# Transposing dqkv for the dxn loop by DMA from SBUF, three tiles ahead, in place of PE

## The chip, the cores and the metric

One core of one Trainium2 chip runs the whole program. The metric is the device time of one execution in microseconds (us), as a median over several executions. The profiles are single executions; their span is 1.7 to 1.9 us shorter than the device time of the same execution. PE is the matmul engine, DVE the vector engine, ACT the scalar engine, SP the engine that only issues DMAs here; SPq and ACTq are the DMA-issuing entries of SP and ACT.

## The reference

The forward pass and the gradients of one pre-layernorm block: linear attention, then a SwiGLU MLP, with 2048 rows and a width of 640 (`S`, `D`). Outputs are the block's result and the gradients of the input and of five weights.

```python
def _fwd_reference(A_x, A_wqkv, A_wo, B_x, B_w1, B_w3, B_w2):
    ...
    x = A_x
    h = x + _A_ref(_layernorm(x, axis=-1), A_wqkv, A_wo)
    h2 = h + _B_ref(_layernorm(h, axis=-1), B_w1, B_w3, B_w2)
    return h2

def reference(A_x, A_wqkv, A_wo, B_w1, B_w3, B_w2, B_x, grad_out):
    ...
    _out, _vjp = jax.vjp(_f, A_x, A_wqkv, A_wo, B_w1, B_w3, B_w2)
    _grads = _vjp(grad_out)
    return (jnp.asarray(_out), *[jnp.asarray(_g) for _g in _grads])
```

The change concerns one product of the backward pass: dxn = dqkv · wqkvᵀ, with dqkv of 2048 x 1920, followed by the backward of the first layernorm.

## The kernel before

The gradients of q, k and v lie in SBUF as `g_q`, `g_k`, `g_v`, in 16 tiles of 128 rows. For dxn the contraction runs over the 1920 columns, so each tile has to be transposed: 15 blocks of 128 x 128. PE transposes five blocks into a PSUM tile, ACT (q and v) or DVE (k) copies them into `gT`. The transposes of tile t+1 stand between the 30 matmuls of tile t. One weight-gradient job of 16 matmuls (`grad_job`) stands ahead of each tile as long as there are any: 20 jobs, 6 of them ahead of the loop, so tiles 14 and 15 have none.

```python
    for i in range(SC):
        dma(out=hnN[:, i * TPC:(i + 1) * TPC, :], in_=hn_v[:, i * TPC:(i + 1) * TPC, :])
    load_block(0)
    load_block(1)
    gT = {}

    def e_T(t, k):
        if k == 0:
            gT[t] = ex.tile([P, 15, P], BF16, name="gT", bufs=2)
        tr = ps.tile([P, DT, P], BF16, name="trq", bufs=2)
        for c in range(DT):
            T.transpose(tr[:, c, :], gqkv[k][:, t, c * P:(c + 1) * P], ident[:])
        if k == 1:
            V.tensor_copy(out=gT[t][:, k * DT:(k + 1) * DT, :], in_=tr[:])
        else:
            A.copy(out=gT[t][:, k * DT:(k + 1) * DT, :], in_=tr[:])

    def e_gxn(t):
        acc = ps.tile([P, 2, 512], F32, name="gxn", tag="gxn", bufs=2)
        for j in range(2):
            for k in range(15):
                T.matmul(acc[:, j, 0:HD], lhsT=gT[t][:, k, :], rhs=wqT[:, k, j * HD:(j + 1) * HD],
                         start=(k == 0), stop=(k == 14))
                if j * 15 + k in (7, 15, 23) and t + 1 < ST:
                    e_T(t + 1, (j * 15 + k) // 8)
        gx = ex.tile([P, D], BF16, name="gx", bufs=2)
        ln_bwd(acc, t, xnN[:, t, :], ln1, gx[:], g_h[:, t, :], ex)()   # ACT sum, DVE, ACT scale, DVE add
        A.dma_start(out=out1S[:, t, :], in_=gx[:])
    # ... pools ...
    for k in range(3):
        next(jobs)
        next(jobs)
        e_T(0, k)
    for t in range(ST):
        next(jobs, None)
        e_gxn(t)
    # ... last stage: 60 jobs with hnN and the blocks gb, load_block(i + 2) at block i ...
```

## Time and profile before

| | before |
|---|---|
| device time, median of 3 | 919.74 us |
| span of the profile | 917.3 us |
| PE / DVE / ACT busy | 96% / 49% / 42% |
| dxn stage, first g_k job to first gb job (PE timeline) | 673.4 to 796.5 us, 123.1 us |
| PE per tile in the loop | 7.08 us |

The busy shares say that PE bounds the program. They do not say how close another engine is: ACT waits inside its sequence of a tile (2.01 us for DVE in the lines that are cut below), and a wait is not counted as busy. The timeline of ACT in one tile of the loop shows this (columns: start in us, length in us, engine, line, operation, output and input, count; in brackets the idle time before it and what ended it):

```profile
744.15 0.70 ACT L636 ACTIVATE gs<-gxn 128x640 bf16<-128x640 f32 x1
...
749.64 1.47 ACT L891 COPY gT<-trq 128x640 bf16<-128x640 bf16 x2 [0.41 <-ACT obs L800]
751.23 0.70 ACT L636 ACTIVATE gs<-gxn 128x640 bf16<-128x640 f32 x1
```

From one sum `gs` to the next it is 7.08 us, PE's pace, but after the two copies ACT stands idle for only 751.23 - 749.64 - 1.47 = 0.12 us. Of the 7.08 us it is busy 3.5; the rest are the waits for DVE in the middle of the layernorm backward and the issue of two stores.

### The profile page before, as it was taken

What the parts mean: (1) busy time and instruction counts of PE and PEld (TensorE: products, weight loads), DVE (VectorE), ACT (ScalarE), POOL (GpSimd) and SP (SyncE); (2) the same over time, 40 slices, a digit from 0 to 9 for tenths busy, and PEclk for the clock granted to TensorE, in tenths of its full rate; (3) what the DMA queues carried; (4) which work ended last, traced back from release to release, by engine and by line L of the source; (5) the groups of instructions that cost most, each with busy time, mean ns of one, the idle gap of its engine ahead of it and who ended that gap; (6) DMA issues with size and microseconds to landing.
All of it is one profiled execution on the core that took longest, in us unless ns stands there. A gap on an engine that the chain in (4) does not pass through costs nothing.

```text
span 917.3 us, 16861 instructions
## 1 busy us (share of the span) xinstructions
PE 883.4 (96%) x6729; PEld 611.5 (67%) x6757; DVE 449.0 (49%) x1146; ACT 388.7 (42%) x722; POOL 22.5 (2%) x42
## 2 busy tenths in 40 slices
PE   5999899999999999899999999999899999999998
PEld 3777554555555555677677777777677777777776
DVE  6776688888888677200145655555323443400000
ACT  3556777665565665011123223223334545422211
POOL 4000000000000000000000000000000000000000
PEclk9999999999999999999999999999999999999999
DMA  9678583353343552999444555148996011066861
GB/s 297 188 246 258 147 240 119 99 141 108 99 136 115 176 168 93 230 224 265 133 134 125 153 163 144 37 165 174 219 275 153 33 40 38 28 153 150 178 149 37
DMA packets 272447, 138.33 MB, mean 151 GB/s; under 512 B 173808, under 2 KB 271088, under 8 KB 272368
## 3 DMA queue, kind: packets, MB, share of 16 engines
q1 hardware_dynamic: 253856, 124.05, 51.8%
q10 hardware_dynamic: 18512, 13.20, 4.6%
q8 instruction: 53, 0.87, 0.4%
q14 instruction: 26, 0.21, 0.1%
HBM read 45.20 MB, written 50.02 MB: 104 GB/s over the span
## 4 chain that ended last, share of the span: by engine, by line
PE 82%; DVE 2%; DMA 2%; ACT 2%; issue 1%; ACTq 0%; DVEq 0%
PE job L796 20%; PE mm L400 19%; PE ghn L625 13%; PE gxn L897 7%; PE gw L559 7%; PE o L448 5%; PE h L675 2%; PE at L361 2%; PE gwo L716 2%; DMA hb<-hh_d 2%; PE trq L887 1%; DMA vaT<-va_d 1%; PE dkv L702 1%; PE h L702 1%; PE h1b L687 1%
## 5 line engine op out<-in xcount | busy, mean ns | idle before, releaser
L400 PE MATMUL mm<-hnT,w 128*128 128x512 bf16 x546 | 132.7, 379 | 1.7 <-ACT hnT L395 1.0
L796 PE MATMUL job<-gb,hnN 128*128 128x288 bf16 x960 | 117.8, 286 | 0.0
L796 PEld LDWEIGHTS <-hnN 128*128 128x128 bf16 x960 | 93.9, 98 | 23.7
L625 PEld LDWEIGHTS <-ggb 128*128 128x128 bf16 x864 | 82.4, 98 | 30.2 <-issue 0.5
L400 PEld LDWEIGHTS <-w 128*128 128x128 bf16 x560 | 53.8, 98 | 61.3 <-issue 1.1
L800 ACT CAST obs<-job 128x288 bf16<-128x288 f32 (+1 forms) x90 | 36.8, 409 | 132.9 <-PE job L796 88.0
L897 PE MATMUL gxn<-wqT,gT 128*128 128x320 bf16 x480 | 74.8, 299 | 0.0
L400 PE MATMUL mm<-g2T,w2T 128*128 128x512 bf16 x266 | 68.3, 379 | 0.8
L448 PE MATMUL o<-w,hhT 128*128 128x320 bf16 x448 | 67.9, 299 | 1.0 <-DVE h L453 1.0
L625 PE MATMUL ghn<-w13a,ggb 128*128 128x320 bf16 x448 | 67.8, 299 | 0.0
L559 PE MATMUL gw<-g,hb 128*128 128x320 bf16 (+1 forms) x448 | 61.1, 299 | 1.3 <-DMA hb<-hh_d 1.3
L219 PE MATMUL big<-wqkv,pqT 128*128 128x320 bf16 x400 | 59.6, 305 | 2.7 <-DVE kvacc L258 1.0
L625 PE MATMUL ghn<-w13b,ggb 128*128 128x320 bf16 x416 | 61.2, 299 | 0.0
L448 PEld LDWEIGHTS <-hhT 128*128 128x128 bf16 x448 | 43.8, 98 | 24.9 <-issue 1.2
L219 PEld LDWEIGHTS <-pqT 128*128 128x128 bf16 x480 | 46.4, 99 | 20.8 <-DVE kvacc L258 1.3
L412 ACT CAST ghh<-mm 128x512 bf16<-128x512 f32 x56 | 32.9, 588 | 63.3 <-issue 39.3
L796 PEld LDWEIGHTS <-xnN 128*128 128x128 bf16 x480 | 47.2, 99 | 18.5
L559 PEld LDWEIGHTS <-hb 128*128 128x128 bf16 (+1 forms) x448 | 44.1, 99 | 18.4 <-DMA hb<-hh_d 1.7
L897 PEld LDWEIGHTS <-gT 128*128 128x128 bf16 x480 | 45.1, 98 | 14.8
L636 ACT ACTIVATE gs<-ghn 128x640 bf16<-128x640 f32 x16 | 11.3, 705 | 95.8 <-PE ghn L625 95.8
L648 ACT ACTIVATE y<-wb,s,ln_rs 128x640 bf16<-128x640 f32 x32 | 29.4, 920 | 40.9 <-DVE wb L644 40.9
L420 ACT ACTIVATE sig<-mm 128x512 bf16<-128x512 f32 x56 | 33.4, 597 | 24.8 <-PE mm L400 24.1
(136 smaller groups left out, 1212.0 us busy)
## 6 DMA issues: line engine op xcount, KB each, us to landing
ggb<-gg_d SPq DMA_DIRECT2D x8, 1728.0 KB, 9.5
hh_d<-hhT SPq DMA_DIRECT2D x52, 128.0 KB, 1.8
gg_d<-gate SPq DMA_DIRECT2D x52, 128.0 KB, 1.9
gg_d<-sig SPq DMA_DIRECT2D x52, 128.0 KB, 1.8
out_dram<-obs ACTq DMA_DIRECT2D x60, 72.0 KB, 2.7
w<-in_B_w_dram SPq DMA_DIRECT2D x4, 864.0 KB, 5.5
va_d<-va SPq DMA_DIRECT2D x4, 768.0 KB, 6.5
out_dram<-gw2o ACTq DMA_DIRECT2D x18, 160.0 KB, 4.7
```

Of the source, the lines that this page charges most:

```text
L219: T.matmul(acc, lhsT=pqT[:, c, t * P:(t + 1) * P], rhs=wqkv[:, c, n0:n0 + HD], start=(c == 0), stop=(c == DT - 1))
L361: T.matmul(at[:, 0:HD], lhsT=oT[t][:, c, :], rhs=wo[:, c, j * HD:(j + 1) * HD], start=(c == 0 and not on_pe), stop=(c == DT - 1))
L400: T.matmul(acc[:], lhsT=w[:, c, fc * P:(fc + 1) * P], rhs=rhs[:, c, :], start=(c == 0), stop=(c == DT - 1))
L412: A.copy(out=ghh[fc][:], in_=acc[:])
L420: A.activation(sig[:], gp[:], AF.Sigmoid)
L448: T.matmul(o2["ps"][:, 0:HD], lhsT=hhT[c][:, fc, i * P:(i + 1) * P], rhs=w2[:, fc, j * HD:(j + 1) * HD], start=(fc == 0), stop=(fc == FT - 1))
L559: T.matmul(acc[:n, j, 0:HD], lhsT=hb[b][:, t, i * P:i * P + n], rhs=g2[:, t, j * HD:(j + 1) * HD], start=(t == 0), stop=(t == ST - 1))
L625: T.matmul(acc[:, j, 0:HD], lhsT=ggb[t // 2][:, k, lo:lo + P], rhs=rhs[:, j * HD:(j + 1) * HD], start=(k == 0), stop=(k == NG - 1))
L648: A.activation(out=y[:], in_=wb[:], func=AF.Identity, bias=s[:, 3:4], scale=st.rs[:, t:t + 1])
L796: T.matmul(acc[:, 0:n], lhsT=lhs[:, t, m * P:(m + 1) * P], rhs=rhs(t), start=(t == 0), stop=(t == ST - 1))
L800: A.copy(out=ob, in_=acc[:, 0:n])
L897: T.matmul(acc[:, j, 0:HD], lhsT=gT[t][:, k, :], rhs=wqT[:, k, j * HD:(j + 1) * HD], start=(k == 0), stop=(k == 14))
```

## The change

Its intent: PE is the bound and the DMA engines are nearly idle in this loop, so let a DMA transpose g_q, g_k and g_v from SBUF straight into `gT`, early enough to be hidden. `gT` gets a third buffer, tile t+3 is transposed after tile t, and the loads for the last stage move from ahead of the loop into it, so that they do not delay the first transposes. Two more switches in the diff (the same idea in two other loops) are off and change nothing; their hunks are cut.

```diff
+TR_A, TR_B, TR_E = 0, 0, 1
 ...
-    for i in range(SC):
-        dma(out=hnN[:, i * TPC:(i + 1) * TPC, :], in_=hn_v[:, i * TPC:(i + 1) * TPC, :])
-    load_block(0)
-    load_block(1)
+    def load_hnN():
+        for i in range(SC):
+            dma(out=hnN[:, i * TPC:(i + 1) * TPC, :], in_=hn_v[:, i * TPC:(i + 1) * TPC, :])
+
+    if not TR_E:
+        load_hnN()
+        load_block(0)
+        load_block(1)
 ...
-            gT[t] = ex.tile([P, 15, P], BF16, name="gT", bufs=2)
+            gT[t] = ex.tile([P, 15, P], BF16, name="gT", bufs=3 if TR_E else 2)
+        if TR_E:
+            dmaT(out=gT[t][:, k * DT:(k + 1) * DT, :], in_=gqkv[k][:, t, :])
+            return
 ...
-                if j * 15 + k in (7, 15, 23) and t + 1 < ST:
+                if j * 15 + k in (7, 15, 23) and t + 1 < ST and not TR_E:
 ...
+    if TR_E:
+        for t in (1, 2):
+            for k in range(3):
+                e_T(t, k)
+        load_hnN()
     for t in range(ST):
         next(jobs, None)
         e_gxn(t)
+        if TR_E:
+            for k in range(3):
+                if t + 3 < ST:
+                    e_T(t + 3, k)
+            if t in (5, 9, 13):
+                load_block((t - 5) // 4)
 ...
-        load_block(i + 2)
+        load_block(i + 2 + TR_E)
```

More of the change, by code (lines that the diff above doesn't have):

```diff
@@ L346, in f2_ot @@
     def f2_ot(t):
+        if TR_A and t >= TPC:
+            o_t, oT[t] = oT[t], pf.tile([P, DT, P], BF16, name="oT", bufs=2)
+            dmaT(out=oT[t][:], in_=o_t[:])
+            return
         tr = ps.tile([P, DT, P], BF16, name="tr", bufs=1)
@@ L391, in f2_ht @@
             hnT[c] = pf.tile([P, DT, W], BF16, name="hnT", bufs=2)
+        if TR_A and t >= TPC:
+            dmaT(out=hnT[c][:, :, i * P:(i + 1) * P], in_=hn[t][:])
+            return
         tr = ps.tile([P, DT, P], BF16, name="tr", bufs=1)
@@ L481 @@
     for i in range(TPC):
-        for k, pos, f in ((3 * i, 0, f2_ndo), (3 * i + 1, 1, f2_ot), (3 * i + 2, 1, f2_at), (3 * i + 3, 0, f2_hn),
-                          (3 * i + 4, 0, f2_ht)):
+        for k, pos, f in ((3 * i, 0, f2_ndo), (3 * i + (not TR_A), 1, f2_ot), (3 * i + 2, 1, f2_at),
+                          (3 * i + 3, 0, f2_hn), (3 * i + 3 + (not TR_A), TR_A, f2_ht)):
             side[pos].setdefault(k, []).append((f, i))
@@ L653, in b_ln, with by_dma @@
         ln_rest[t] = ln_bwd(acc, t, hnb[t][:], ln2, g_h[:, t, :], g2[:, t, :], br)
+    def by_dma(t):
+        return TR_B and t < ST - 2
     def b_gT(t):
+        if by_dma(t):
+            ghT[t] = br.tile([P, DT, P], BF16, name="ghT", bufs=2)
+            dmaT(out=ghT[t][:], in_=g_h[:, t, :])
+            return
         tr = h1b(DT)
@@ L684, in b_gndT @@
     def b_gndT(t):
+        if by_dma(t):
+            gndT[t] = br.tile([P, CT, P], BF16, name="gndT", bufs=2)
+            dmaT(out=gndT[t][:], in_=gnd[t][:])
+            return
         tr = h1b(CT)
@@ L742 @@
             load_gg(t // 2 + 1)
-        if 0 <= u < ST:
+        if 0 <= u < ST and not by_dma(u):
             b_gT(u)
@@ L748 @@
         if w >= 0:
-            b_gndT(w)
-            b_gkv(w)
+            if not by_dma(w):
+                b_gndT(w)
+            if not TR_B:
+                b_gkv(w)
         part()
-        if 0 <= u < ST:
+        if 0 <= u < ST and not TR_B:
             b_go(u)
@@ L756 @@
             ln_rest.pop(t - 1)()
+            if by_dma(t - 1):
+                b_gT(t - 1)
+        if w >= 0 and TR_B:
+            b_gkv(w)
         part()
-        if w >= 0:
+        if 0 <= u < ST and TR_B:
+            b_go(u)
+        if w >= 0 and not TR_B:
             b_gpq(w)
@@ L761 @@
         part()
+        if w >= 0 and TR_B:
+            b_gpq(w)
+        if 0 <= u < ST and by_dma(u):
+            b_gndT(u)
         if t == ST:
@@ L883, in e_T @@
         if k == 0:
-            gT[t] = ex.tile([P, 15, P], BF16, name="gT", bufs=2)
+            gT[t] = ex.tile([P, 15, P], BF16, name="gT", bufs=3 if TR_E else 2)
+        if TR_E:
+            dmaT(out=gT[t][:, k * DT:(k + 1) * DT, :], in_=gqkv[k][:, t, :])
+            return
         tr = ps.tile([P, DT, P], BF16, name="trq", bufs=2)
```

## The prediction

> **What bounds the kernel now.** I read the page first (busy shares, slices, DMA), then the PE timeline and the groups by shape of the stage that the change touches, then who waited for whom there, then the DMA queue. The change touches one stage only: the dxn loop (16 tiles, L897) with the six weight-gradient jobs ahead of it. The order of instructions of the two builds differs in nothing else that can matter: PE loses 480 of 13,516 rows (240 transposes with their weight loads), ACT 32 copies, DVE 16 copies, SP gains 48 transposes and has the loads of hnN and of the first gb blocks later; the kernel's two other switches are off.
>
> ```profile
> PE 883.4 (96%) x6729; PEld 611.5 (67%) x6757; DVE 449.0 (49%) x1146; ACT 388.7 (42%) x722; POOL 22.5 (2%) x42
> ...
> PE   5999899999999999899999999999899999999998
> ...
> DMA  9678583353343552999444555148996011066861
> ```
>
> PE is busy for 96% of the span and nine tenths or more in nearly every slice, while the DMA engines have four almost empty slices, 30 to 34 (some 690 to 800 us): the dxn loop. One tile of it, and its last two, from the PE timeline (start, length, what; the bracket is idle time with its releaser):
>
> ```profile
> 708.52 2.34 PE L796 MATMUL job<-g_k,xnN 128*128 128x320 bf16 x16
> 710.69 1.25 PE L897 MATMUL gxn<-wqT,gT 128*128 128x320 bf16 x8
> 711.78 0.44 PE L887 MATMUL trq<-ident,g_q 128*128 128x128 bf16 x5
> 712.06 1.25 PE L897 MATMUL gxn<-wqT,gT 128*128 128x320 bf16 x8
> ...
> 715.60 2.34 PE L796 MATMUL job<-g_v,xnN 128*128 128x320 bf16 x16
> ```
>
> ```profile
> 789.19 1.25 PE L897 MATMUL gxn<-wqT,gT 128*128 128x320 bf16 x8
> 791.36 0.44 PE L887 MATMUL trq<-ident,g_v 128*128 128x128 bf16 x5 [0.92 <-DVE gT L889]
> 791.64 5.05 PE L897 MATMUL gxn<-wqT,gT 128*128 128x320 bf16 x36
> ```
>
> Lengths overlap because matmuls are pipelined, so costs are read from one start to the next. Five transposes: 712.06 - 711.78 = 0.28 us. A job of 16: 710.69 - 708.52 = 2.17. Eight gxn: 1.09, 0.136 each. A tile: 715.60 - 708.52 = 7.08 us = 2.17 + 30 x 0.136 + 3 x 0.276. Nothing else is in it: PE is the bound, with no gap. The only wait of PE from 673 to 797 us is the bracket above: the last tiles have no job between them, and there a transpose waits for the copy that frees its PSUM buffer.
>
> The copies beside it, by shape, are not on the path:
>
> ```profile
> L891 ACT COPY gT<-trq 128x640 bf16<-128x640 bf16 x32 | 21.9, 692 | 11.3 <-ACT obs L800 6.7 <-PE trq L887 3.0 <-DVE gT L889 0.9
> ...
> L889 DVE COPY gT<-trq 128x640 bf16<-128x640 bf16 x16 | 7.9, 491 | 26.0 <-PE trq L887 26.0
> ```
>
> ACT and DVE are busy 3.53 and 2.89 us of the 7.10 us of this tile in the busy time by stretches, and wait between pieces. Taking their copies away gives time only through PE.
>
> **What the Trainium skill says.** "TensorE: Matmul & The Clock Gate", Part 4 (PE-mode transpose): a 128x128 transpose was measured at about 390 ns alone and 275 ns in a kernel. The trace has 219 ns as the length of one, but pipelined five start within 0.276 us, 55 ns each; the saving must be counted by the 55. The skill's figure or the 219 ns would promise 53 to 66 us for 240 of them, four times too much.
> "DMA: Bandwidth & Descriptors", Latency and other measured facts: DMA transposes move 261 GB/s with a non-contiguous middle dimension. Here 1.18 MB of a gb block take 4.84 us to issue (244 GB/s) and land after 7.7 us; that agrees.
> Same page, the passage on the B0 build under "Why a DMA increments its semaphore by 16 and not by 1": before that build, an SBUF-to-SBUF transpose of 8,192 tiles took 262,144 sequencer cycles, one push command per tile, so 32 cycles per tile. It does not say how large a tile is. No SBUF-to-SBUF transpose is in the trace of before, so this is the one open cost.
>
> **What a transposing DMA costs here.** Two rows of the issues, and their queue entries:
>
> ```profile
> gb<-gg_d SPq DMA_TRANSPOSE x12, 7.7
> ...
> pqT<-pq_d SPq DMA_TRANSPOSE x4, 5.5
> ```
>
> ```profile
> L874 SPq DMA_TRANSPOSE gb<-gg_d x12: 4727/4844/11370, 676.2 to 884.9; - x12
> ```
>
> ```profile
> L193 SPq DMA_TRANSPOSE pqT<-pq_d x4: 2687/2737/2860, 49.7 to 108.2; - x4
> ```
>
> A block of gb is 288 x 2048, 4608 pieces of 256 bytes (128 bf16); pqT is 512 x 640, 2560 pieces. The queue is held 4.84 and 2.74 us: (4.84 - 2.74) / 2048 = 1.03 ns per piece and 0.1 us fixed. Landing comes 2.8 to 2.9 us after the issue ends. A gT piece is 128 x 640, 640 pieces: estimate 0.76 us of queue, landing 3.6 us after its start. DMA engine time: from 810 to 850 us their share is 0.67 to 0.71, about 0.11 of it the output stores (share of the loop now); 0.57 x 9.8 us for one gb block is 5.6 us of all engines, so 0.78 us for a gT piece. The two estimates agree. If the skill's 32 cycles hold for a tile of 16 x 128 (40 in a piece) at the 1.2 GHz that its front page "Trainium Kernel Development and Optimization"[...] gives for SyncEngine, it is 1.07 us.
>
> **The change part by part.**
> 1. Removed from PE, on the path: 48 groups of five transposes x 0.276 us = 13.2 us. Three of these groups stood between the jobs ahead of the loop, 45 in it.
> 2. Removed: the stall of the last tiles, 1.1 us (791.36 less 790.28, when the eight gxn begun at 789.19 had all been passed).
> 3. Removed beside PE: 32 ACT copies (21.9 us) and 16 DVE copies (7.9 us): 0.
> 4. Added: 48 DMA transposes of 160 KB on the SP queue. gT has three buffers; that of tile t+3 is free when tile t's gxn end and is needed two tiles and a job later. A tile will take 7.08 - 0.83 = 6.25 us, so the deadline is 2 x 6.25 + 2.17 = 14.7 us. Three transposes need 2 x 0.76 + 3.6 = 5.1 us by the estimate, 5.8 us at 1.07 us each. Hidden, with some 9 us to spare: 0.
> 5. The first tile: SP is free at 673.4 us, when the six jobs begin, and gT of tile 0 is wanted 7 x 2.17 = 15.2 us later. Ready in 5: 0.
> 6. Moved: hnN and gb blocks 0 to 2 load within the loop, whose DMA is idle. Four tiles with a gb block need 12 x 0.78 + 5.6 = 15 us of DMA in 25 us. The last stage (796.5 us on) still finds its blocks loaded, and from then on a block waits for the same buffer as before: 0.
>
> Sum: -13.2 - 1.1 = -14.3 us. Check of the stage: it lasts from 673.4 to 796.5, 123.1 us; 20 jobs x 2.17 + 480 x 0.136 = 108.8 us are left, 14.3 less. 919.7 - 14.3 = 905.4; I say 905.5.
>
> **The rivals.**
> (a) The SP queue or the DMA engines become the bound of the loop. Needed: three transposes in over 6.25 us, 2.1 us each, or 1.6 us each in the four-tile groups with a gb block of 5.6 us. For: [...]the speed from DRAM may not carry over, and a tile in the skill's sense may be smaller than 16 x 128. Against: it takes twice to three times my estimates. At 3 us each, 48 x 3 + 3 x 5 = 159 us for the stage against 123 before: 955 us. At 2 us: 111 us, about 908.
> (b) A wait for a late gT or a DMA semaphore shared with the output stores takes the place of part of the transposes: a few tenths per tile, 2 to 6 us, 908 to 912. For: the new issues carry waits on earlier DMAs, the stores of ACT among them; gx goes out 4.4 us after its tile and lands 1.8 us on, just a tile later. Against: 9 us of slack.
> (c) Nothing gained, because ACT and DVE set the pace at 6.25 us per tile. Against: without their copies they are busy some 2.2 and 2.4 us of it; the chain of sums and scaling takes about 4 us and has two buffers. Would give 919; hardly possible.
>
> **Range and chances.** The gain on PE is nearly certain and cannot be more than 14.3 us (1.6%), so faster by 2% (under 901.3) has 0.02. All hidden, 904.5 to 906.5: about 0.75. Rival (b) or a mild (a): 0.12. Slower by 2% (over 938) needs over 2.5 us per transpose: 0.09. Range 903.5 to 914.
>
> **What would show each step right or wrong.** Right: no trq group; a tile of 6.25 us in the PE timeline; PE waits for no gT; the stage lasts about 109 us; 48 gT transposes of under 1.1 us of queue time each, landing in about 4 us; DMA share in the loop up from 0.11 to about 0.5 to 0.6. Wrong: PE or its weight loads idle before L897 with gT's DMA as releaser, transposes back to back on SP all through the loop, or tiles longer than 6.3 us.

## The result and the profile after

The changed kernel takes 906.65 us (median of 4, 906.53 to 907.07) against 919.86 us of the kernel before in the same rounds. The ratio is 0.9857, with a 95% interval of 0.984 to 0.9874: faster by 1.4%, so within the 2% band. Ratios are the mean time of one kernel's fast runs over that of the other's of the same rounds, so not quite the ratio of the medians quoted.

Slices of the page after (40 slices of 22.6 us, busy share in tenths):

```profile
PE   5999899999999999999999999999899999999998
...
DMA  9688483343343373799845444426999588666751
```

The empty DMA slices of the dxn loop are filled, to an extent that the prediction did not expect: in stretches of 25 us (726.4 to 751.4 and 751.4 to 776.4) the DMA share is 0.84 and 0.92, against 0.11 before. PE's row is the same but for one digit. The PE timeline of one tile and of the end of the loop after:

```profile
713.92 2.34 PE L827 MATMUL job<-g_v,xnN 128*128 128x320 bf16 x16
716.09 4.24 PE L935 MATMUL gxn<-wqT,gT 128*128 128x320 bf16 x30
720.17 2.34 PE L827 MATMUL job<-g_v,xnN 128*128 128x320 bf16 x16
...
772.33 12.39 PE L935 MATMUL gxn<-wqT,gT 128*128 128x320 bf16 x90
784.55 15.72 PE L827 MATMUL job<-gb,hnN 128*128 128x288 bf16 x127
```

A tile takes 720.17 - 713.92 = 6.25 us. No line of the loop has a bracket: PE never waits, and the last three tiles run as 90 matmuls in a row. The stage lasts from 675.89 (first g_k job) to 784.55, 108.7 us against 123.1: 14.5 us less. The queue entries of the transposes in the view by tile (duration in ns as minimum/median/maximum, then first and last start):

```profile
L921 SPq DMA_TRANSPOSE gT<-g_q x16: 1199/1201/2344, 673.5 to 770.3; - x16
L921 SPq DMA_TRANSPOSE gT<-g_k x16: 1267/1268/2715, 675.2 to 772.7; - x16
L921 SPq DMA_TRANSPOSE gT<-g_v x16: 1215/1225/1260, 676.6 to 774.1; - x16
```

They hold the queue for 1.20 to 1.27 us each and land 2.8 us after their start (median). ACT in a tile after:

```profile
714.12 0.70 ACT L644 ACTIVATE gs<-gxn 128x640 bf16<-128x640 f32 x1 [1.16 <-PE gxn L935]
...
718.78 0.42 ACT L831 CAST obs<-job 128x320 bf16<-128x320 f32 x1 [0.94 <-DVE gx L657]
...
720.37 0.70 ACT L644 ACTIVATE gs<-gxn 128x640 bf16<-128x640 f32 x1 [1.16 <-PE gxn L935]
```

Without copies ACT waits 1.16 us for PE at the head of each sequence. It has more room at 6.25 us than it had at 7.08.

The stage gives 14.5 us in this trace and the medians differ by 13.2. The stages ahead, whose instructions are the same, ended 2.5 us later in this execution (675.9 against 673.4). The first experiment asks whether that is chance.

### The profile page after: what moved, and what is told of

The parts are those of the page before. It is cut to its first block, busy times and chain, and to the rows that moved or that the text cites. A ratio compares the mean times of both kernels' runs of the same rounds, so it can differ in the third digit from the quotient of the medians.

```text
span 905.3 us, 16415 instructions
## 1 busy us (share of the span) xinstructions
PE 871.9 (96%) x6489; PEld 599.4 (66%) x6517; DVE 441.7 (49%) x1130; ACT 366.5 (40%) x690; POOL 22.4 (2%) x42
## 4 chain that ended last, share of the span: by engine, by line
PE 82%; DMA 3%; DVE 2%; ACT 2%; issue 1%; ACTq 0%; DVEq 0%; SPq 0%
PE job L827 20%; PE mm L408 19%; PE ghn L633 13%; PE gxn L935 7%; PE gw L567 7%; PE o L456 5%; PE h L690 2%; PE at L366 2%; PE gwo L735 2%; DMA hb<-hh_d 1%; DMA vaT<-va_d 1%; PE dkv L721 1%; PE h L721 1%; PE h1b L706 1%; PE nd L329 1%
## 5 line engine op out<-in xcount | busy, mean ns | idle before, releaser
L935 PE MATMUL gxn<-wqT,gT 128*128 128x320 bf16 x480 | 67.5, 299 | 0.0
L935 PEld LDWEIGHTS <-gT 128*128 128x128 bf16 x480 | 47.0, 98 | 18.2
```

## The experiments

All runs gave correct results except `from_dram`. The first four shared a chip, the next four another, the last four a third; each group has its own runs of the kernel before. "Stage" is the time from the first g_k job to the first gb job in the run's PE timeline.

| run | median us | before, same group | stage us |
|---|---|---|---|
| after_again | 907.28 | 920.6 | 109.7 |
| pe_back | 919.93 | 920.6 | 122.1 |
| copies_back | 922.35 | 920.6 | 123.9 |
| late_loads | 922.15 | 920.6 | 123.1 |
| from_dram (one look) | 905.58 | 920.73 | 110.1 |
| sizes (one look) | 927.53 | 920.73 | 128.4 |
| double | 953.56 | 920.73 | 156.1 |
| ahead2 | 907.51 | 920.73 | 108.8 |
| copies_clean | 914.11 | 920.15 | 113.3 |
| tra / trb / trab | 912.6 / 906.1 / 910.58 | 920.15 | 108.7 in each |

### after_again: the changed kernel once more

No edit.

> The changed kernel unchanged, once more, for a tight ratio and a second trace. Its dxn stage (from the first g_k job to the first gb job) was 108.7 us in the trace against 123.1 before, 14.5 less, yet the medians differ by 13.2 only and the stage began 2.5 us later in the profiled run (675.9 against 673.4). Theory 1, spread between executions in the stages ahead: this trace begins the stage nearer to 673.4 to 675 and lasts 108.7 again, and the median is 905.4 to 906.7. Theory 2, the new code costs something ahead of the stage: it begins at 675.5 to 676 again and the median is 906.6 to 907.

Measured: 907.28 us (905.74 to 908.81), ratio 0.9853 (0.9833 to 0.9873). This trace starts the stage at 676.6, later still. By the terms set beforehand that is nearer to theory 2, though the median is above both ranges. But over all the traces whose stages ahead have the same instructions, but for 5 or 10 transposes that set up the two runs with copies (the two kernels and the experiments down to `copies_clean`), the start lies anywhere from 672.9 to 677.3 us, and the latest one, `late_loads`, is an edit of the kernel before. So the start spreads by 4.4 us between executions; that the changed code costs something there is not supported. The stage was 1.0 us longer than in the first trace, and the PE timeline shows why:

```profile
688.03 0.42 ACT L831 CAST obs<-job 128x320 bf16<-128x320 f32 x1 [3.48 <-PE job L827]
688.51 2.33 PE L827 MATMUL job<-g_k,xnN 128*128 128x320 bf16 x16 [0.89 <-ACT obs L831]
```

A job waited for PSUM, because ACT copied the one before it 3.48 us late. The bracket names PE, which had long been done. ACT's queue was held at the store issued just before: the copy of the job before it ended at 684.55, its store was issued at 687.64. In the built program the DMAs of both queues take eight completion semaphores in turn, and the next user of one waits for the one before; three of the stores ahead of the loop wait in this way for gT transposes that stand eight DMAs before them, though they need nothing from them. This is the prediction's rival (b), at 0.9 us. The same wait of PE ahead of the loop is in three more traces with these transposes (`copies_back` 0.8, `from_dram` 1.2, `double` 1.3 us), is 4.8 us in `sizes`, and is absent from the others, the first trace of the changed kernel among them: it comes and goes between executions.

### pe_back: only PE's transposes come back

```diff
+    def e_dead(t, k):                      # at the old places; nobody reads the result
+        tr = ps.tile([P, DT, P], BF16, name="trq", bufs=2)
+        for c in range(DT):
+            T.transpose(tr[:, c, :], gqkv[k][:, t, c * P:(c + 1) * P], ident[:])
```

> Changed kernel, with the 48 groups of five PE transposes put back at their old places, into a PSUM tile that nobody reads; no copies; gT still comes by DMA. My theory (the gain is PE time, 0.276 us a group, 13.2 us in all): 906.7 + 13.2 = 919.9 us, within 1 us, and the tile is 7.08 us again. Rival (the gain came from freeing ACT and DVE of their copies): within 2 us of 906.7.

Measured: 919.93 us, 12.65 us above the changed kernel of the same group, ratio to the kernel before 0.9991 (0.9975 to 1.0008). The transposes cost what was predicted:

```profile
720.81 0.44 PE L934 MATMUL trq<-ident,g_q 128*128 128x128 bf16 x5
721.09 1.25 PE L940 MATMUL gxn<-wqT,gT 128*128 128x320 bf16 x8
```

Again 0.28 us from the start of five to the next matmul. PE time is enough to explain all the gain, and the DMA transposes beside it cost nothing that can be seen. Seen from the other side, the run is the kernel before with DMA transposes in place of the copies: as long as PE's transposes stay, taking the copies away is worth next to nothing (the stage is 1.0 us shorter, the stall of the last tiles).

### copies_back and copies_clean: only the copies come back

`copies_back` puts back the 32 ACT and 16 DVE copies at the old places, from one PSUM tile, with no PE transposes in the loop.

```diff
+    def e_copy(k):
+        if k == 1:
+            V.tensor_copy(out=kvbd[:, :, P:2 * P], in_=trc[:])
+        else:
+            A.copy(out=kvbd[:, :, 0:P], in_=trc[:])
```

> Changed kernel, with the 32 ACT and 16 DVE copies of 128x640 put back at their old places, from one PSUM tile filled once, into a dead SBUF tile; no PE transposes. My theory (the copies were beside the path): 906.7 us within 1 us. Rival (the copies mattered, ACT or DVE sets the pace of a 6.25 us tile): 910 to 920. A small rise of about 1 us at the last two tiles, which have no job between them, would fit the stall of 1.1 us seen before.

Measured: 922.35 us (921.99 to 923.87). My expectation failed by 15 us: the copies alone undid the whole gain, in a stage of 123.9 us. The trace shows PE waiting for ACT's `gs` at every gxn from tile 8 on. But it also shows a fault of the experiment: since ACT and DVE share the tiles, the DVE copy waited 2 us for ACT's first copy and ACT's second 0.56 us for DVE. The kernel before has no such waits, so the run proves too much. `copies_clean` gives each engine its own PSUM source and its own dead SBUF tile.

```diff
-            V.tensor_copy(out=kvbd[:, :, P:2 * P], in_=trc[:])
+            V.tensor_copy(out=mask[:, :, 0:P], in_=trd[:])
-            A.copy(out=kvbd[:, :, 0:P], in_=trc[:])
+            A.copy(out=kvbd[:, :, k * P:(k + 1) * P], in_=trc[:])
```

> The first run with the copies put back took 922.4 us against my 906.7, but its ACT and DVE copies waited for each other (0.56 and 2 us), which the kernel before does not have. Here each engine copies from its own PSUM tile to its own dead SBUF tile, so ACT runs the old sequence (sum, scale, job copy, two gT copies in a row) without those waits. New theory (in the kernel before ACT's in-order sequence of one tile was nearly as long as PE's 7.08 us: from 779.58 to 786.54, 6.96 us, so the copies had to go too): a tile falls from 6.25 to about 7.0 us after the PSUM buffers are used up, the stage takes 115 to 118 us instead of 108.7 to 109.7, the time is 912 to 917 us, and PE waits for ACT before gxn. Old theory (copies beside the path, the first run's loss was only its extra waits): 906 to 909.

Measured: 914.11 us (912.64 to 917.34). The changed kernel did not run in this group; against the kernel before of each group it gains 6.0 us, where the changed kernel gained 13.2 and 13.3. ACT's timeline:

```profile
739.89 0.72 ACT L644 ACTIVATE gs<-gxn 128x640 bf16<-128x640 f32 x1
...
745.41 1.29 ACT L935 COPY kvbd<-trc 128x640 bf16<-128x640 bf16 x2 [0.41 <-ACT obs L831]
746.58 0.72 ACT L644 ACTIVATE gs<-gxn 128x640 bf16<-128x640 f32 x1
```

One sequence with copies and with no idle time at its end takes 746.58 - 739.89 = 6.69 us. That is less than my 7.0, as the second copy no longer waits for PE, but it is more than PE's 6.25. ACT falls back by 0.44 us a tile; over 14 tiles that is 6.2 us. The two PSUM buffers hide it until the end, where PE pays it in large pieces:

```profile
780.91 5.91 PE L941 MATMUL gxn<-wqT,gT 128*128 128x320 bf16 x30 [2.44 <-ACT gs L644]
786.65 2.12 PE L827 MATMUL job<-gb,hnN 128*128 128x288 bf16 x16
791.48 8.69 PE L827 MATMUL job<-gb,hnN 128*128 128x288 bf16 x56 [2.70 <-ACT gs L644]
```

So 0.18 (tile 14, not shown), 2.44 and 2.70 us of waiting, the last after the stage's nominal end, plus 1.7 us because the 30 matmuls after the 2.44 us gap took 5.91 us in place of 4.24, at a granted clock of 0.70 (the share of full TensorE clock that the profile shows). The matmuls after the 2.70 us gap ran slower too, at 0.80 from 791.5 to 800.2 us: 56 took 8.69 us where 0.1226 us each from start to start, as elsewhere in that stage, would make 6.9. Together these pieces are some 8.8 us in this trace; the medians show a loss of about 7. What follows: ACT was a second bound close below PE. A change that took away only PE's transposes and left the copies would, by this run, have kept about half of the gain (6.0 of 13.2 to 13.3 us).

### late_loads: only the moved loads

The kernel before, with the loads of hnN and of gb blocks 0 to 2 moved as the change moves them.

```diff
-    (hnN and load_block(0), load_block(1) ahead of the jobs)
+    (hnN after the first transposes)
         e_gxn(t)
+        if t in (5, 9, 13):
+            load_block((t - 5) // 4)
```

> The kernel before, with only the loads moved as the change moves them: hnN after the first transposes, gb blocks 0 to 2 after tiles 5, 9 and 13. Result stays right. My theory (the move is worth nothing by itself, DMA was not on the path at that place): 919.9 us within 1 us. Rival (crowded DMA at 673 to 700 us, share over 1.0, cost something that the move removed): 917 to 918.5.

Measured: 922.15 us (920.08 to 923.11), ratio 1.0011 (0.9991 to 1.0031), stage 123.1 us as before. The median is outside my 1 us, but the trace puts all of it ahead of the stage, which began at 677.3 us. The move is worth nothing by itself. That it makes room for the transposes is argued, not shown: no run has the transposes without it.

### from_dram and sizes: what does a transpose cost?

`from_dram` takes each piece from rows of a DRAM tensor of the same shape (wrong data).

```diff
-            dmaT(out=gT[t][:, k * DT:(k + 1) * DT, :], in_=gqkv[k][:, t, :])
+            dmaT(out=gT[t][:, k * DT:(k + 1) * DT, :], in_=(pq_d, pk_d, hn_d)[k][t * P:(t + 1) * P, :])
```

> Changed kernel, but each gT piece is transposed from rows of a DRAM tensor of the same 128 x 640 shape (wrong result on purpose: other data). Measured so far: a piece from SBUF holds the queue for 1.20 to 1.27 us, against my estimate of 0.76 from the large DRAM transposes, and takes about 1.27 us of all DMA engines against 0.78. If the SBUF source is what costs more: here 0.7 to 0.85 us of queue a piece and a DMA share in a tile without a gb block of about 0.5. If a small transpose costs a fixed part that the large ones hide: 1.2 us again and a share of about 0.7. The time is the same, 906 to 907.5, by both.

`sizes` splits the k piece into 256 and 384 columns and the v piece into 128 and 512.

```diff
+            for a, b in (((0, 5),), ((0, 2), (2, 5)), ((0, 1), (1, 5)))[k]:
+                dmaT(out=gT[t][:, k * DT + a:k * DT + b, :], in_=gqkv[k][:, t, a * P:b * P])
```

> Changed kernel, with the g_k piece split into 256 and 384 columns and the g_v piece into 128 and 512, g_q left at 640: five transposes a tile instead of three, the same bytes. Result stays right. If the 1.2 us of a 640 piece is proportional to size (1.9 ns per 256 bytes): 0.25, 0.5, 0.75, 1.0 us of queue for 128, 256, 384, 512 columns, and the loop is unchanged. If it has a fixed part of some 0.5 us: 0.65, 0.8, 0.95, 1.1 us. Time 906 to 908 by both, as 5 us a tile is still under 6.25.

Queue entries of `from_dram`, one of the three groups, and of `sizes`, all three, in the view by tile:

```profile
L921 SPq DMA_TRANSPOSE gT<-pq_d x16: 1199/1200/2274, 673.0 to 768.8; - x16
```

```profile
L922 SPq DMA_TRANSPOSE gT<-g_k x32: 1236/1247/2489, 676.3 to 797.2; - x32
L922 SPq DMA_TRANSPOSE gT<-g_v x32: 1119/1197/2081, 678.9 to 799.9; - x32
L922 SPq DMA_TRANSPOSE gT<-g_q x16: 1200/1220/1917, 674.3 to 794.7; - x16
```

For the queue time the source does not matter: 1.20 us from DRAM too (the other two groups 1.27 and 1.28), which is the second of the two expectations; landing took longer, 3.5 us against 2.8 (medians). The size does not matter either, from 128 to 640 columns: all five sizes take 1.12 us or more. Taken one by one in the order of issue, the records of `sizes` have medians of 1.18, 1.24, 1.25, 1.21 and 1.22 us for 128, 256, 384, 512 and 640 columns. So a transposing DMA of 128 rows holds the queue for about 1.2 us up to 160 KB, where the line through the large ones (0.1 us and 1.03 ns per 256 bytes) gave 0.76. Neither of the two expectations of `sizes` had this: one scaled with size, the other had a smaller fixed part. Whether the floor is one per DMA or comes from the 128 rows is open; no run has a small transpose with another number of rows.

The time of `sizes`, 927.53 us in one look, follows from it: five DMAs of about 1.25 us are the whole tile (6.5 us from one tile's first piece to the next, 710.85 to 717.36), and the gb blocks come on top. It was the queue that was full and not the DMA engines: in that stretch their share was 0.43. PE waited 3.6 us for gT, and 8.5 us in two stalls (4.79 and 3.75 us) for ACT, whose job copies were held as in `after_again`; after each stall the next 16 matmuls took 4.4 us in place of 2.34, at a granted clock of 0.50.

### double: each piece twice

```diff
             dmaT(out=gT[t][:, k * DT:(k + 1) * DT, :], in_=gqkv[k][:, t, :])
+            for k2 in range(3 if k == 2 else 0):
+                dmaT(out=gT[t][:, k2 * DT:(k2 + 1) * DT, :], in_=gqkv[k2][:, t, :])
```

> Changed kernel, with each gT piece transposed twice into the same place (result stays right): 6 transposes of about 1.25 us a tile. Theory (transposes on the one queue cost 1.25 us each in series and were hidden only because 3 x 1.25 = 3.75 us is under 6.25): the queue becomes the bound, a tile takes 7.5 us and more with a gb block of 5.3 us in between; the queue ends its last gT at about 673.5 + 96 x 1.25 + 2 x 5.3 + 3 = 807 us instead of 775, so some 30 us longer, 930 to 942. Rival (transposes run beside each other on 16 engines and the queue time is only issue): under 912.

Measured: 953.56 us (950.79 to 956.82), ratio 1.0351. From tile 3 on PE now waits for gT in every tile but one:

```profile
744.81 2.34 PE L827 MATMUL job<-g_k,xnN 128*128 128x320 bf16 x16
747.36 0.85 PE L937 MATMUL gxn<-wqT,gT 128*128 128x320 bf16 x5 [0.21 <-DMA gT<-g_q]
```

In this part of the loop six pieces follow each other on the queue every 8.0 us (starts at 716.46 and 724.52), 1.34 each with the gaps between, so the direction and the mechanism are as expected and the size is not: I had 1.25 each, and had left out that the pieces beside the hnN load take 2.2 us each. The transposes do not run beside each other in a way that would hide them; the queue serves them in series (the DMA share from 716.46 to 724.52 is 0.78, so the engines were not full), and the change works because three of them take 3.75 us of 6.25.

### ahead2: two buffers

```diff
-gT[t] = ex.tile([P, 15, P], BF16, name="gT", bufs=3 if TR_E else 2)
+gT[t] = ex.tile([P, 15, P], BF16, name="gT", bufs=2)
-                if t + 3 < ST:
-                    e_T(t + 3, k)
+                if t + 2 < ST:
+                    e_T(t + 2, k)
```

> Changed kernel with two gT buffers, transposed two tiles ahead instead of three. The time from a free buffer to its use falls from 14.7 to 6.25 + 2.17 = 8.4 us; three pieces take 3 x 1.25 + 1.6 = 5.4 us, so tiles without a gb block stay hidden. After a gb block (5.3 us of queue) the next tile is short by 1 to 2 us at most, three times. Theory: 906.7 to 910. Rival (three buffers are needed, DMA landing is late in general): over 915.

Measured: 907.51 us (905.17 to 909.6), ratio 0.985 (0.9817 to 0.9882), stage 108.8 us with no wait of PE in the loop. The third buffer is not needed in this loop.

### tra, trb, trab: the same idea elsewhere

These turn on the diff's two other switches, to see whether a version beats both kernels: A in the forward loop (24 groups of five transposes), B in the ghn loop (14 tiles of 5 + 6).

```diff
-TR_A, TR_B, TR_E = 0, 0, 1
+TR_A, TR_B, TR_E = 1, 0, 1        # tra; 0, 1, 1 is trb and 1, 1, 1 is trab
```

> Changed kernel with the same idea in the forward loop (switch A on: hn and o of tiles 4 to 15 transposed by DMA, 24 groups of five). PE saving 24 x 0.276 = 6.6 us if hidden; PE there is 98 to 99% busy. If hidden: 900 us. If the transposes (1.25 us of queue each, behind the stores of the same queue, landing after 2.8 us or more) come too late for their users one or two steps on: 907 us or more.

> Changed kernel with the same idea in the ghn loop (switch B on: 14 tiles, 5 + 6 transposes each). PE saving 14 x 11 x 0.055 = 8.5 us if hidden; PE there is 100% busy and the DMA share 0.40 to 0.45. If hidden: 898 us. If late or if the order of the loop makes PE wait: 905 us or more.

> Both switches on. If both are hidden and add up: 906.7 - 6.6 - 8.5 = 891.6 us, 889 to 894. If one is not: the other's time.

Measured: 912.6 us (ratio 0.9911), 906.1 us (0.9847, interval 0.9831 to 0.9864) and 910.58 us (0.9898). None is clear of the changed kernel's 0.9853 and 0.9857 for the better. The hoped-for gains failed to come: `tra` and `trb` fell in the second branch of their expectations (907 or more, 905 or more), and `trab` lies between those two runs. The waits of PE in `tra`:

```profile
PE at L366 <- DMA oT<-o_t: 10.3, 7, 4.6
...
PE mm L408 <- DMA hnT<-hn: 2.7, 2, 2.3
```

In the forward loop the transposed tile is used one or two steps later, and PE waits 13.0 us for the two transposes together, twice the 6.6 us that could be saved. In `trb` PE waits 2.2 us for ghT, 3.4 us at the end of the loop and 2.5 us after it, and the clock is 0.94 from 600 to 672 us (0.95 in the trace of the changed kernel). The ghn loop gained about 6 us (its last ghn matmul began at 595.4 us against 601.3, and the loop began at 447.9 against 448.0 us), and the two waits after it gave about as much back. I did not take this apart further.

## Why the prediction was right, point by point

- **The bound and its price per transpose.** Right. A tile is 6.25 us as worked out, and `pe_back` shows that 48 groups put back cost 12.65 us (13.2 predicted).
- **The stall of the last tiles.** Right: the 90 matmuls in a row have no gap.
- **The sum.** 14.3 us predicted for the stage; 14.5 and 13.4 in the two traces of the changed kernel. For the time: 905.5 predicted, 906.65 and 907.28 measured, just above the 904.5 to 906.5 that it gave for all hidden and below rival (b)'s 908. Against the kernel before of the same rounds the gain is 13.2 and 13.3, so 1.0 to 1.1 us are missing. One trace shows 0.9 us as the rival (b): ACT's stores behind the transposes' semaphores, ahead of the loop. The first trace has no such wait, and there the difference lies in the stages ahead; how much of it is spread is not settled.
- **Step 3, the copies are worth nothing.** Right beside PE's 7.08 us (`pe_back`, which has no copies, takes 919.93 against 920.6), but incomplete, without harm to the number. "Not on the path" was read from busy times; that the 13.2 us of step 1 need the copies gone as well was not seen. `copies_clean` shows that ACT's sequence with copies takes 6.69 us, more than the 6.25 us of the new tile, and costs some 7 us of the gain if it stays. The change took both loads away at once, so my sum held by luck in this term. Rival (c), which has the copies gone, was rightly put aside: ACT waits 1.16 us for PE in each tile after.
- **Step 4, the cost of a transpose.** The mechanism (in series on one queue, hidden by a deadline of 14.7 us) was right, shown by `double` and `ahead2`. The term was mis-sized: 0.76 us predicted, 1.20 to 1.27 measured, because the line through large transposes does not hold for small ones. The 1.07 us worked out from the skill's cycles per tile came nearer by chance: it grows with the number of tiles, and in `sizes` the queue time does not. (The 1.2 GHz in it stands under NeuronCore Architecture on that front page.) Landing came after 2.8 us, not 3.6. Three pieces are ready 2 x 1.25 + 2.8 = 5.3 us after their buffer is free, by chance close to the predicted 5.1.
- **Step 5, the first tile.** Right: its last piece started at 676.57 us and PE's first gxn at 691.10, without a wait.
- **Step 6, the moved loads.** Right, by `late_loads`, and the last stage lasts 120.8 us in both traces. But the DMA share went to 0.84 and 0.92 with the blocks of gb, not to 0.5 to 0.6: there was less room on the engines than I said. What `sizes` ran out of was queue time, though, with a DMA share of 0.43 to 0.54 in its tiles from 710 to 745 us.
- **A reading.** The four almost empty DMA slices before are 31 to 34 (711 to 803 us); slice 30 has a 6, from the loads of hnN and gb. Nothing in the sum rests on it.

## What to carry to other kernels

When work is moved off the bounding engine, look at the whole sequence of each engine beside it, waits included, not at its busy share: here ACT, 42% busy over the program, had 0.12 us of idle at the end of a 7.08 us tile and would have been the next bound. Price a DMA transpose by its count as well as by its bytes (about 1.2 us of queue for 128 rows, whatever the width up to 640 columns), and check that the sum per iteration, other transposes included, stays under the iteration. Then ask how long after the data exists the user needs it: the same trade gained 13 us where there were two tiles to spare, and lost 5 us in the forward loop, where there were one or two steps.

## What the Trainium skill lacked or had wrong

- "DMA: Bandwidth & Descriptors", Latency and other measured facts, gives a bandwidth for DMA transposes that small ones do not reach. Here a transpose of 128 rows holds the queue for 1.2 us with 128 columns as with 640, from SBUF as from DRAM, and 640 columns in 1.2 us are 137 GB/s (163,840 bytes), about half of the page's 261 GB/s; the large gb blocks agree with the page (244 GB/s). The skill does have a figure for small ones: the page's table on the B0 build gives a cost per instruction for small tiles from HBM, one row above the row that the prediction used, and the prediction passed over it.
- The same page, the passage on the B0 build, gives the older SBUF-to-SBUF transposes as 32 cycles per tile. In `sizes` the queue time does not follow the number of tiles of any fixed size: 128 and 512 columns take 1.18 and 1.21 us.
- "TensorE: Matmul & The Clock Gate", Part 4, gives 275 ns for a PE transpose in a kernel. As a length the trace has 219 ns; as a cost, five in a row take 0.276 us. Part 4 does not separate the two, and for the worth of removing one they differ by four times.
- The same page, Why this matters for your kernels, warns of PE gaps above about 3 us. In `copies_clean` a gap of 2.44 us was followed by a clock of 0.70 over the next 5.7 us. The length alone does not decide here: after a gap of 2.55 us in `trb` (before 633.46 us) the clock stayed at 1.00.
